# Later pairs' outputs transposed by VectorE in 32x32 blocks instead of by TensorE, in a fused attention and mixture-of-experts kernel

## The chip, the cores and the metric

The kernel runs on one core of one Trainium2 chip. The metric is device time in microseconds (us) of one execution. Before the change it is 1516.14 us, the median of 3 runs (1514.83 to 1516.44).

## The reference

Attention inside chunks of 64 tokens, then a mixture of four experts over the 4608 x 512 result, all in fp32:

```python
def _attn_ref(q, k, v):                       # (8, 8, 576, 64) each
    ...
    scores = scale * np.matmul(q_c, k_c.transpose(0, 1, 2, 4, 3))   # chunks of 64
    attn = softmax(scores)
    out = np.matmul(attn, v_c)

def _moe_ref(x, domain_probs, w1, w2):        # x (4608, 512), w1 (4, 512, 1024), w2 (4, 1024, 512)
    p = domain_probs / (domain_probs.sum(-1, keepdims=True) + 1e-09)
    for e in range(E):
        h = np.maximum(x @ w1[e], 0.0)
        out += p[:, e:e + 1] * (h @ w2[e])
```

## The kernel before

The 4608 tokens are cut into nine subs of 512 (`SUB`). The first sub is done alone, the other eight as four pairs, numbered 0 to 3. Each expert's hidden layer is cut in two halves, so there are eight passes (`n_pass`) over the weights per sub or pair: passes 0 to 7 for the first sub, 8 to 15 for pair 0, and 16 to 39 for pairs 1, 2 and 3, "the later pairs", eight each. Every fp32 factor is split into a high and a low part, and a product of two tiles is six TensorE instructions (two blocks of the inner dimension times high x high, low x high and high x low), all issued at L465 in `product`. The two products of a pair of subs use a scheme with seven products in place of eight; names such as "a11", "s1", "t4" are its sums of blocks.

In a later pair a pass is woven by hand (`WOVEN`): 28 steps, each one product. `g1` to `g7` and `h1` to `h7` make the hidden layer of this pass, from weights w1; `a1` to `a7` and `b1` to `b7` multiply the hidden layer of the pass before by w2. Their results are added by VectorE (L694) into eight SBUF tiles `acc0` to `acc7`, of 128 output columns by 512 tokens each: `acc[m + 4 s]` is the block of columns m (0 to 3) of sub s (0 or 1) of the pair. The accumulators are thus transposed against the output, which has tokens in rows. Group a makes the blocks with even m, group b those with odd m.

When a pair is done, its accumulators are transposed and stored. For pairs 1 and 2 that is woven into the first pass of the next pair and into the pass after (`outputs`, called from `later_pass`): four calls behind steps 15, 18, 21 and 24 of passes 24 and 32 for even m, and four behind steps 1, 4, 7 and 10 of passes 25 and 33 for odd m. Each call has TensorE transpose four 128x128 pieces into the PSUM tile `psa` (L780), ScalarE copy them to a stage (`e` or `pt`, L789), and SP issue two stores of 128 KB, in rows of 512 bytes (L793). The last pair has no next pass; `last_products` runs its fourteen w2 steps in the order `ALONE`, and transposes between them with `plane`: seven blocks as whole planes (four transposes, a copy by ScalarE or VectorE at L1331, a store at L1333) and the eighth, of which the last product is computed in two halves of 256 tokens (`by_halves`).

All transfers are issued by SP from one queue, in the order in which the program is written. Most are the weight factors of the later pairs: `ring_load` (L370) brings 512 KB into one of six SBUF tiles `wf0` to `wf5`, three for w1 and three for w2; the tile is used by two steps for each of its two units, and when the last of these is done it is loaded again with the unit three further on in its ring. GpSimd (POOL) makes the low parts of the hidden layer (L647), ScalarE the high parts (L644), VectorE the ReLU with the expert's share (L632) and the sums (L638, L667).

Of the kernel before, what the change touches and what calls it, by code (L numbers as in the profile page):

```python
# [8 lines left out]
F32 = mybir.dt.float32  # L9
# [6 lines left out]
P = 128  # L16
C = 64
SUB = 512
NT = SUB // P
HG = 4  # L20
GT = 2
NK = 4
# [3 lines left out]
PAIR = 2  # L26
# [4 lines left out]
def chunk_attention_moe(ctx: ExitStack, tc: tile.TileContext, qk, v, v0, dp, w1, w2, out):  # L31
# [10 lines left out]
    nc = tc.nc  # L42
# [9 lines left out]
    att = ctx.enter_context(tc.tile_pool(name="att", bufs=1))  # L52
# [6 lines left out]
    ps = ctx.enter_context(tc.tile_pool(name="ps", bufs=1, space=bass.MemoryType.PSUM))  # L59
# [5 lines left out]
    def bank(name=None):  # L65
        if name is None:
            name = BANKS[turn[0] % len(BANKS)]
            turn[0] += 1
        return ps.tile([P, SUB], F32, name=name)
# [40 lines left out]
    st = {}  # L110
# [368 lines left out]
    acc = {}  # L479
# [190 lines left out]
    class Outer:  # L670
# [17 lines left out]
        def add(self, src, i, s):  # L688
            key = self.n // n_pass, 2 * i + self.g + NK * s
            if key not in acc:  # L690
                acc[key] = opool.tile([P, SUB], F32, name=f"acc{key[1]}")
                nc.scalar.copy(out=acc[key], in_=src)
            else:
                nc.vector.tensor_tensor(out=acc[key], in0=src, in1=acc[key], op=ALU.add)  # L694
# [32 lines left out]
    class Tile:  # L727
# [25 lines left out]
        def whole(self):  # L753
            self.part(range(NK), slice(0, dm), True, True)
# [22 lines left out]
    def output_part(pair, i, m, out_ps):  # L777

        s, j = divmod(i, NT)
        nc.tensor.transpose(out_ps, acc[pair + 1, m + NK * s][:, j * P : (j + 1) * P], ident)  # L780

    def outputs(pair, i, g):

        ps = psa[:, 0].rearrange("p (i m d) -> p i m d", i=2, d=P)
        for j in range(2):
            for m in range(2):
                output_part(pair, i + j, g + 2 * m, ps[:, j, m])
        stage = att.tile([P, 2, 2, P], F32, name=("e", "pt")[i // 2 % 2])
        nc.scalar.copy(out=stage, in_=ps)  # L789
        t = (1 + pair * PAIR) * NT + i  # L790
        to = out[t * P : (t + 2) * P, :].rearrange("(i p) (m d) -> p i m d", p=P, d=P)
        for j in range(2):
            nc.sync.dma_start(out=to[:, j, g::2], in_=stage[:, j])  # L793


    scr = xpool.tile([P, NK * PAIR * SUB], F32, name="xraw")
# [386 lines left out]
        1: ((LATE, 0),), 2: ((EARLY, 1),), 3: ((EARLY, 2), (LATE, 3)), 4: ((EARLY, 4),),  # L1183
        5: ((EARLY, 5), (LATE, 6)), 6: ((EARLY, 7),),
    }
    ALONE = "a1 b1 a2 a5 b5 a6 b6 a3 b3 a7 b7 b2 a4 b4".split()

    def first_load(pair):
        if pair < n_pairs:
# [51 lines left out]
    def later_pass(n, ahead, late, held):  # L1241

        first_pass, last_pass = n % n_pass == 0, n % n_pass == n_pass - 1
        pair, more = n // n_pass - 1, n + 1 < n_run
        at = {}
        left, sc = Units(n), Scaled(n)
        steps = {"gh"[g]: LaterGroup(g, left, sc, False) for g in range(2)}
        steps |= {"ab"[g]: Outer(g, n - 1, ahead[1], ahead[0], False) for g in range(2)}

        def put(i, name, k, of=sc):  # L1250
            add(at, i, lambda: of.hi(name, k), lambda: of.lo(name, k))

        for f in held:
            add(at, 0, f)
        second_half(at, ahead[0])
        for i, f in late:
            add(at, i, f)

        add(at, 12, lambda: sc.sum("t3", 0, nc.gpsimd))
        put(16, "b11", 0)  # L1260
        put(16, "b11", 1)
        add(at, 18, lambda: sc.sum("t2", 0))
        put(19, "t2", 0)
        put(20, "b22", 0)
        add(at, 22, lambda: sc.sum("t1", 0))
        put(22, "t3", 0)
        put(23, "t1", 0)
        put(24, "b21", 0)
        put(24, "b22", 1)
        put(26, "b21", 1)  # L1270
        if more:
            add(at, 26, lambda: sc.sum("t4", 0, nc.gpsimd))
        add(at, 27, lambda: sc.sum("t1", 1), lambda: sc.sum("t3", 1))
        if n % 2 and more:
            add(at, 13, lambda: probs_load(n + 1, 0))
            add(at, 27, lambda: probs_load(n + 1, 1))
        if pair + 1 < n_pairs:
            for places, i in TILES.get(n % n_pass, ()):
                attend(at, pair + 1, places, i)
        late = []  # L1280
        if first_pass and pair > 1:
            for i in range(4):
                add(at, 15 + 3 * i, lambda i=i: outputs(pair - 1, 2 * i, 0))
            late = [(1 + 3 * i, lambda i=i: outputs(pair - 1, 2 * i, 1)) for i in range(4)]
        if last_pass and more:
            x = Tokens(pair + 1)
            add(at, 5, x.sum1)
            add(at, 8, lambda: x.sum3(nc.gpsimd), lambda: x.sum2_apart(nc.gpsimd))
            add(at, 13, x.sum4_apart)
            add(at, 15, lambda: x.hi("b11"))  # L1290
            add(at, 16, lambda: x.hi("b21"), lambda: x.lo("b11"))
            add(at, 18, lambda: x.lo("b21"))
            add(at, 20, x.split2)
            add(at, 23, lambda: x.hi("t1"))
            add(at, 24, lambda: x.lo("t1"))
            add(at, 25, lambda: x.hi("t3"))
            add(at, 26, lambda: x.hi("t4"))
            late = [
                (0, lambda: x.hi("b22")), (0, lambda: first_load(pair + 2)), (1, lambda: x.lo("t3")),
                (6, lambda: x.lo("t4")), (8, lambda: x.lo("b22")),  # L1300
            ]
        for i, name in enumerate(WOVEN):
            getattr(steps[name[0]], f"p{name[1]}")()
            for f in at.get(i, ()):
                f()
        return (sc, left), late, ()
# [11 lines left out]
    def last_products(ahead):  # L1318

        pair, at = n_pairs - 1, {}  # L1320
        second_half(at, ahead[0])
        add(at, 2, lambda: ahead[0].sum("t4", 0, nc.gpsimd))
        steps = {"ab"[g]: Outer(g, n_run - 1, ahead[1], ahead[0], True) for g in range(2)}
        stages = [(hpool, f"s{i}", 1) for i in (1, 2, 3)]
        stages += [(wpool, "wraw", N_RAW)] * 4 + [(att, "e", 1), (att, "pt", 1)]

        def store(s, m, ps, eng, rows=range(NT)):

            pool, name, bufs = stages.pop()
            stage = pool.tile([P, len(rows), P], F32, name=name, bufs=bufs)  # L1330
            eng(out=stage, in_=ps)  # L1331
            t = (1 + pair * PAIR + s) * NT + rows[0]
            nc.sync.dma_start(  # L1333
                out=out[t * P : (t + len(rows)) * P, m * P : (m + 1) * P].rearrange("(i p) d -> p i d", p=P),
                in_=stage,
            )

        def plane(s, m, ps, eng):
            ps = ps.rearrange("p (i d) -> p i d", d=P)
            for j in range(NT):  # L1340
                output_part(pair, s * NT + j, m, ps[:, j])
            store(s, m, ps, eng)

        def by_halves(o):

            left, n = o.left(1, "a22", o.g), SUB // 2
            sums = []
            for i, ps in enumerate((psa[:, 1], bank("A0"))):
                cols = slice(i * n, (i + 1) * n)
                product(ps[:, :n], PARTS, lambda k, a: left[a][:, k], lambda k, b: o.h.part("t4", b)[:, k, cols])  # L1350
                sums.append(opool.tile([P, n], F32, name=f"acc{NK + i}"))
                nc.vector.tensor_tensor(
                    out=sums[i], in0=ps[:, :n], in1=acc[o.n // n_pass, 2 + o.g][:, cols], op=ALU.add
                )
            for i, ps in enumerate((bank("A1"), bank("B1"))):
                ps = ps[:, :n].rearrange("p (i d) -> p i d", d=P)
                for j in range(n // P):
                    nc.tensor.transpose(ps[:, j], sums[i][:, j * P : (j + 1) * P], ident)
                store(0, 2 + o.g, ps, (nc.scalar.copy, nc.vector.tensor_copy)[i], range(2 * i, 2 * i + 2))

        act, dve = nc.scalar.copy, nc.vector.tensor_copy
        for i, name in enumerate(ALONE[:-1]):
            getattr(steps[name[0]], f"p{name[1]}")()
            for f in at.get(i, ()):
                f()
            if name == "b7":
                steps["b"].add(steps["b"].a, 1, 0)
            elif name == "b2":
                plane(1, 0, bank("C1"), act)
                plane(1, 1, bank("C0"), act)  # L1370
            elif name == "a4":
                plane(1, 2, psa[:, 0], act)
                plane(1, 3, bank("B1"), dve)
                plane(0, 0, bank("B0"), act)
                plane(0, 1, bank("C1"), dve)
                plane(0, 2, bank("C0"), act)
        by_halves(steps["b"])

    with tc.manual_schedule():
# [58 lines left out]
```

## Time and profile before

| | |
|---|---|
| runs shown | 1514.83, 1516.14, 1516.44 us (median 1516.14) |
| the profiled execution | 1515.59 us, of which the span from first to last instruction is 1513.8 us |
| TensorE (PE) | busy 1505.7 us, 99% of the span, 8854 matmuls |
| VectorE (DVE), ScalarE (ACT), GpSimd (POOL) | busy 918.6, 572.9, 871.7 us: 61%, 38%, 58% |
| transfers | 314.17 MB in 167936 packets, mean 208 GB/s; the SP queue's packets take 63.7% of the 16 DMA engines' time |
| granted TensorE clock | 1.00 |

The profile is of one execution, 0.55 us faster than the median of the runs shown. A matmul's row gives its own duration, but matmuls overlap: six of 128x512 follow each other in 1.36 us. The chain of work that ended last gives time without this overlap. "Packets" are the pieces of a transfer, one for each contiguous run of bytes. A group's row has its count, its busy time and the mean duration of one.

### The profile page before, as it was taken

The numbers are of one execution on the slowest core, as the hardware profiler recorded it, in microseconds if no ns is written. First come the engines' busy times: TensorE is split into PE (matmuls) and PEld (weight loads), VectorE is DVE, ScalarE is ACT, GpSimd is POOL, SyncE is SP. The second block draws the span as 40 slices with busy tenths as digits, with TensorE's granted clock in tenths as the row PEclk, the third lists the DMA queues.
The fourth block names the chain that finished last, engine by engine and source line by source line (L and its number), as shares of the span: only waits on it lengthen the run. The fifth ranks groups of instructions, "written<-read, shape, count | busy, mean of one in ns | idle before, by whom it ended". The sixth has DMA issues, their size and how long they took to land.

```text
span 1513.8 us, 23370 instructions
## 1 busy us (share of the span) xinstructions
PE 1505.7 (99%) x8854; PEld 1238.8 (82%) x8855; DVE 918.6 (61%) x1289; ACT 572.9 (38%) x1000; POOL 871.7 (58%) x666
## 2 busy tenths in 40 slices
PE   9999999999999999999999999999999999999998
PEld 7888888888888888888888888888888888888887
DVE  5443554444444465776766956666668756666665
ACT  3333444344444334333333444333333443333332
POOL 2443588677766616555556754555557555555554
PEclk9999999999999999999999999999999999999999
DMA  6443359877767576767665677676666676666664
GB/s 197 133 156 125 106 167 310 274 251 243 231 234 238 187 266 215 230 209 228 205 203 189 216 226 243 205 229 209 212 190 200 204 231 201 201 200 201 200 191 145
DMA packets 167936, 314.17 MB, mean 208 GB/s; under 512 B 14208, under 2 KB 84112, under 8 KB 167824
## 3 DMA queue, kind: packets, MB, share of 16 engines
q1 hardware_dynamic: 167824, 312.68, 63.7%
q8 instruction: 70, 1.15, 0.3%
q14 instruction: 42, 0.34, 0.1%
HBM read 244.39 MB, written 68.23 MB: 207 GB/s over the span
## 4 chain that ended last, share of the span: by engine, by line
PE 99%; DVE 0%; ACT 0%; issue 0%; ACTq 0%
PE A L465 49%; PE C L465 29%; PE B L465 16%; PE psa L169 1%; PE psa L140 1%; PE psa L160 1%; PE psa L780 0%; PE C L901 0%; PE B L852 0%; PE A L832 0%; PE C L780 0%; PE A L852 0%; PE psa L832 0%; PE B L838 0%; PE psa L838 0%; PE B L780 0%
## 5 line engine op out<-in xcount | busy, mean ns | idle before, releaser
L647 POOL TENSOR_TENSOR hfl<-wraw,hfh 128x512 fp32r<-128x512 f32 x288 | 374.4, 1316 | 216.2 <-ACT hfh L644 214.0
L465 PE MATMUL A<-xh,wf 128*128 128x512 f32 (+1 forms) x1104 | 379.5, 389 | 0.0
L465 PE MATMUL A<-hfh,wf 128*128 128x512 f32 (+1 forms) x768 | 270.6, 394 | 0.0
L644 ACT CAST hfh<-wraw 128x512 fp32r<-128x512 f32 x288 | 176.4, 622 | 208.5 <-DVE wraw L638 59.7
L465 PEld LDWEIGHTS A<-xh,wf 128*128 128x128 f32 x1104 | 206.8, 188 | 43.1
L527 ACT COPY s<-A 128x512 f32<-128x512 f32 x192 | 112.8, 587 | 329.7 <-PE A L465 328.9
L465 PE MATMUL A<-xl,wf 128*128 128x512 f32 (+1 forms) x552 | 213.7, 388 | 0.0
L465 PE MATMUL C<-xh,wf 128*128 128x512 f32 (+1 forms) x600 | 204.0, 388 | 0.7 <-ACT xh L278 0.7
L465 PEld LDWEIGHTS A<-hfh,wf 128*128 128x128 f32 x768 | 144.1, 188 | 31.0 <-DVE acc L694 1.2
L694 DVE TENSOR_TENSOR acc<-A,acc 128x512 f32<-128x512 f32 x174 | 119.2, 686 | 78.7 <-PE A L465 78.2
L465 PE MATMUL A<-hfl,wf 128*128 128x512 f32 x384 | 149.4, 389 | 0.0
L465 PE MATMUL C<-hfh,wf 128*128 128x512 f32 x384 | 133.9, 390 | 0.0
L281 POOL TENSOR_TENSOR hfl<-wraw,hfh 128x512 fp32r<-128x512 f32 x64 | 85.9, 1372 | 80.5 <-ACT hfh L278 80.5
L465 PEld LDWEIGHTS C<-xh,wf 128*128 128x128 f32 x600 | 111.5, 188 | 23.9 <-ACT xh L278 0.8
L465 PE MATMUL B<-xh,wf 128*128 128x512 f32 (+1 forms) x376 | 125.3, 384 | 0.0
L281 POOL TENSOR_TENSOR wf<-wraw,wf 128x512 fp32r<-128x512 f32 x70 | 91.5, 1330 | 53.4 <-ACT wf L278 53.2
L465 PEld LDWEIGHTS A<-xl,wf 128*128 128x128 f32 x552 | 103.5, 188 | 21.1
L465 PE MATMUL C<-xl,wf 128*128 128x512 f32 (+1 forms) x300 | 114.7, 385 | 0.0
L638 POOL TENSOR_TENSOR wf<-wraw,wf 128x512 f32<-128x512 f32 x23 | 29.7, 1291 | 145.2 <-DVE wf L632 145.2
L694 DVE TENSOR_TENSOR acc<-C,acc 128x512 f32<-128x512 f32 x90 | 62.2, 691 | 64.3 <-PE C L465 58.7
L647 POOL TENSOR_TENSOR hfl<-wf,hfh 128x512 fp32r<-128x512 f32 x48 | 71.2, 1483 | 38.9 <-ACT hfh L644 38.6
L465 PEld LDWEIGHTS C<-hfh,wf 128*128 128x128 f32 x384 | 72.1, 188 | 14.9
(186 smaller groups left out, 2727.7 us busy)
## 6 DMA issues: line engine op xcount, KB each, us to landing
wf<-w SPq DMA_DIRECT2D x336, 512.0 KB, 4.1
wraw<-in_w SPq DMA_DIRECT2D x128, 256.0 KB, 4.0
w<-wf SPq DMA_DIRECT2D x112, 256.0 KB, 4.7
qk_in<-in_qk SPq DMA_DIRECT2D x32, 512.0 KB, 5.4
v_in<-in_v SPq DMA_DIRECT2D x32, 256.0 KB, 4.4
w<-hfl SPq DMA_DIRECT2D x32, 256.0 KB, 2.7
w<-hfh SPq DMA_DIRECT2D x32, 256.0 KB, 2.9
w<-hfh SPq DMA_DIRECT2D x48, 128.0 KB, 2.7
```

Source lines behind the costliest of these rows:

```text
L140: nc.tensor.matmul(s["sc"][half, c, j], lhsT=s["x"][rows, g, 0, h], rhs=s["x"][rows, g, 1, h], start=True, stop=True,)
L160: nc.tensor.transpose(ps[:, j], s["e"][:, j].rearrange("p c k -> p (c k)"), ident)
L169: nc.tensor.matmul(av[half, c, j], lhsT=s["v"][rows, 2 * j + odd], rhs=s["pt"][rows, j, half], start=True, stop=True,)
L281: eng.tensor_tensor(out=t[1], in0=src, in1=t[0].bitcast(F32), op=ALU.subtract)
L465: nc.tensor.matmul(out, lhsT=lhs(k, a), rhs=rhs(k, b), start=first and i == 0, stop=last and i == len(parts) - 1, skip_group_check=not (fi ...
L527: nc.scalar.copy(out=t, in_=self.a)
L638: (eng or nc.vector).tensor_tensor(out=self.values[place, k], in0=self.values[a, k], in1=self.values[b, k], op=op)
L644: nc.scalar.copy(out=self.part(name, 0)[:, k], in_=self.values[name, k])
L647: (eng or nc.gpsimd).tensor_tensor(out=self.part(name, 1)[:, k], in0=self.values[name, k], in1=self.part(name, 0)[:, k].bitcast(F32), op=A ...
L694: nc.vector.tensor_tensor(out=acc[key], in0=src, in1=acc[key], op=ALU.add)
```

## The change

The transposes of `outputs` and of three blocks of the tail leave TensorE. VectorE transposes a whole accumulator (128x512) with one instruction that transposes each 32x32 block in itself (`nc.vector.transpose`, L797 and L1339 in the new kernel). The blocks then are still at the wrong place on the block level, and the store puts them right: four transfers per accumulator, one for each group of 32 partitions, in rows of 32 floats (128 bytes) in place of 128 floats (`put_out`, L789 in the new kernel). In the tail three blocks, (s, m) = (0,0), (1,0) and (1,3), go that way; (0,1), (1,2), (1,1), (0,2) and the halved (0,3) stay with TensorE. The order of the w2 steps there (`ALONE`) moves b7 and b2 ahead of a7 and b3, and the transposes of block (0,2) go between the two halves of the last product.

```diff
-    def outputs(pair, i, g):
-
-        ps = psa[:, 0].rearrange("p (i m d) -> p i m d", i=2, d=P)
-        for j in range(2):
-            for m in range(2):
-                output_part(pair, i + j, g + 2 * m, ps[:, j, m])
-        stage = att.tile([P, 2, 2, P], F32, name=("e", "pt")[i // 2 % 2])
-        nc.scalar.copy(out=stage, in_=ps)
-        t = (1 + pair * PAIR) * NT + i
-        to = out[t * P : (t + 2) * P, :].rearrange("(i p) (m d) -> p i m d", p=P, d=P)
-        for j in range(2):
-            nc.sync.dma_start(out=to[:, j, g::2], in_=stage[:, j])
+    B = 32
+
+    def put_out(pair, m, s, stage):
+
+        t = (1 + pair * PAIR + s) * SUB
+        to = out[t : t + SUB, m * P : (m + 1) * P]
+        for a in range(P // B):
+            nc.sync.dma_start(
+                out=to[:, a * B : (a + 1) * B].rearrange("(b i) j -> i b j", i=B),
+                in_=stage[a * B : (a + 1) * B].rearrange("i (b j) -> i b j", j=B),
+            )
+
+    def outputs(pair, m, s):
+
+        stage = att.tile([P, SUB], F32, name=("e", "pt")[s])
+        nc.vector.transpose(stage, acc[pair + 1, m + NK * s])
+        put_out(pair, m, s, stage)
...
-    ALONE = "a1 b1 a2 a5 b5 a6 b6 a3 b3 a7 b7 b2 a4 b4".split()
+    ALONE = "a1 b1 a2 a5 b5 a6 b6 a3 b7 b2 a7 b3 a4 b4".split()
...
             for i in range(4):
-                add(at, 15 + 3 * i, lambda i=i: outputs(pair - 1, 2 * i, 0))
-            late = [(1 + 3 * i, lambda i=i: outputs(pair - 1, 2 * i, 1)) for i in range(4)]
+                add(at, 15 + 3 * i, lambda i=i: outputs(pair - 1, 2 * (i // 2), i % 2))
+            late = [(1 + 3 * i, lambda i=i: outputs(pair - 1, 1 + 2 * (i // 2), i % 2)) for i in range(4)]
...
+        def whole(s, m):
+
+            t = stage(SUB)
+            nc.vector.transpose(t, acc[pair + 1, m + NK * s])
+            put_out(pair, m, s, t)
...
+                if i == 0:
+                    plane(0, 2, bank("C1"), act)
...
+        add(at, 3, lambda: whole(0, 0))
+        add(at, 8, lambda: steps["b"].add(steps["b"].a, 1, 0))
+        add(at, 8, lambda: whole(1, 0))
+        add(at, 9, lambda: whole(1, 3))
+        add(at, 11, lambda: plane(0, 1, psa[:, 0], act))
+        add(at, 12, lambda: plane(1, 2, bank("B0"), act))
+        add(at, 12, lambda: plane(1, 1, bank("C0"), act))
...
-            if name == "b7":
-                steps["b"].add(steps["b"].a, 1, 0)
-            elif name == "b2":
-                plane(1, 0, bank("C1"), act)
-                plane(1, 1, bank("C0"), act)
-            elif name == "a4":
-                plane(1, 2, psa[:, 0], act)
-                plane(1, 3, bank("B1"), dve)
-                plane(0, 0, bank("B0"), act)
-                plane(0, 1, bank("C1"), dve)
-                plane(0, 2, bank("C0"), act)
```

TensorE in pass 24, from the end of step 15 (h2, into bank B0) to step 16 (b1, into A1), before; `psa` is the PSUM tile of the transposes:

```order
L465 MATMUL B0_8526<-xl0_8199,wf0_8441 128x512
L465 MATMUL B0_8526<-xh0_8198,wf0_8441 128x512
L780 MATMUL psa_95<-ident_90,acc0_5723 128x128
L780 MATMUL psa_95<-ident_90,acc2_5889 128x128
L780 MATMUL psa_95<-ident_90,acc0_5723 128x128
L780 MATMUL psa_95<-ident_90,acc2_5889 128x128
L465 MATMUL A1_8544<-hfh0_8211,wf2_8398 128x512
```

Now step 16 follows step 15 with nothing between, there and at the fifteen other places. VectorE from the same step 15 on, now:

```order
L667 TENSOR_TENSOR B0_8526<-B0_8526,s1_8524 128x512
L632 SCALAR_TENSOR_TENSOR wraw_8534<-B0_8526,ws_5471 128x512
L797 STREAM_TRANSPOSE e_8536<-acc0_5723 128x512
L694 TENSOR_TENSOR acc1_5947<-A1_8542,acc1_5947 128x512
L694 TENSOR_TENSOR acc7_5962<-C1_8558,acc7_5962 128x512
L638 TENSOR_TENSOR wraw_8411<-wf6_8505,wraw_8411 128x512
L797 STREAM_TRANSPOSE pt_8577<-acc4_5831 128x512
L694 TENSOR_TENSOR acc5_5989<-A1_8542,acc5_5989 128x512
```

Before, the same rows stood there without the two L797, so each transpose now comes behind the ReLU or sum of its step and ahead of the next accumulations. SP at the same place, before, where `out_0` is the output and `w...` the weight units in memory:

```order
L370 DMA wf4_8522<-w0_0_6_102 128x1024
L793 DMA out_0<-e_8540 256x1x128 x2
L370 DMA wf2_8551<-w7_1_6_207 128x1024
L370 DMA wf0_8574<-w1_0_0_110 128x1024
L793 DMA out_0<-pt_8583 256x1x128 x2
L370 DMA wf5_8593<-w0_1_0_103 128x1024
```

and now:

```order
L370 DMA wf4_8522<-w0_0_6_102 128x1024
L789 DMA out_0<-e_8536 32x16x32 x4
L370 DMA wf2_8549<-w7_1_6_207 128x1024
L370 DMA wf0_8572<-w1_0_0_110 128x1024
L789 DMA out_0<-pt_8577 32x16x32 x4
L370 DMA wf5_8589<-w0_1_0_103 128x1024
```

Two stores have become four at the same places between the weight loads. TensorE in the tail, from the end of the last whole steps to the first half of the last product (into `psa`), before:

```order
L465 MATMUL B0_14002<-hfh1_13865,wf5_13928 128x512
L780 MATMUL C1_14010<-ident_90,acc4_11810 128x128 x4
L780 MATMUL C0_14018<-ident_90,acc5_11953 128x128 x4
L465 MATMUL A1_13902<-hfh3_13967,wf0_13789 128x512
L465 MATMUL A1_13902<-hfl3_13969,wf0_13789 128x512
...
L780 MATMUL psa_95<-ident_90,acc6_11787 128x128 x4
L780 MATMUL B1_14040<-ident_90,acc7_11932 128x128 x4
L780 MATMUL B0_14048<-ident_90,acc0_11715 128x128 x4
L780 MATMUL C1_14056<-ident_90,acc1_11917 128x128 x4
L780 MATMUL C0_14064<-ident_90,acc2_11884 128x128 x4
L465 MATMUL psa_95<-hfh3_13967,wf5_13928 128x256
```

and now, where the step into A1 is a4 again and A0 takes the second half of the last product:

```order
L465 MATMUL C0_13916<-hfh2_13782,wf4_13864 128x512
L1357 MATMUL psa_95<-ident_90,acc1_11885 128x128 x4
L465 MATMUL A1_13870<-hfh3_13941,wf0_13757 128x512
...
L1357 MATMUL B0_14010<-ident_90,acc6_11759 128x128 x4
L1357 MATMUL C0_14018<-ident_90,acc5_11921 128x128 x4
L465 MATMUL psa_95<-hfh3_13941,wf5_13896 128x256
...
L1357 MATMUL C1_14035<-ident_90,acc2_11852 128x128 x4
L465 MATMUL A0_14026<-hfh3_13941,wf5_13896 128x256
```

Seven planes have become four, one of them between the halves. VectorE in the tail now, from step b7 (into A0) on:

```order
L694 TENSOR_TENSOR acc7_11900<-A0_13879,acc7_11900 128x512
L694 TENSOR_TENSOR acc3_11999<-A0_13879,acc3_11999 128x512
L1339 STREAM_TRANSPOSE e_13962<-acc4_11782 128x512
L694 TENSOR_TENSOR acc1_11885<-B0_13968,acc1_11885 128x512
L1339 STREAM_TRANSPOSE wraw_13976<-acc7_11900 128x512
L694 TENSOR_TENSOR acc6_11759<-A1_13870,acc6_11759 128x512
```

The accumulation of step a7, the row with `acc6`, which must be done before step a4 may write on into A1, now has two transposes ahead of it.

More of the change, by code (lines that the diff above doesn't have):

```diff
@@ L1325, in last_products, with stage @@
         stages += [(wpool, "wraw", N_RAW)] * 4 + [(att, "e", 1), (att, "pt", 1)]
+        def stage(*shape):
+            pool, name, bufs = stages.pop()
+            return pool.tile([P, *shape], F32, name=name, bufs=bufs)
+        def whole(s, m):
+            t = stage(SUB)
+            nc.vector.transpose(t, acc[pair + 1, m + NK * s])
+            put_out(pair, m, s, t)
         def store(s, m, ps, eng, rows=range(NT)):
-            pool, name, bufs = stages.pop()
-            stage = pool.tile([P, len(rows), P], F32, name=name, bufs=bufs)
-            eng(out=stage, in_=ps)
+            st = stage(len(rows), P)
+            eng(out=st, in_=ps)
             t = (1 + pair * PAIR + s) * NT + rows[0]
@@ L1334, in store @@
                 out=out[t * P : (t + len(rows)) * P, m * P : (m + 1) * P].rearrange("(i p) d -> p i d", p=P),
-                in_=stage,
+                in_=st,
             )
+        act = nc.scalar.copy
         def plane(s, m, ps, eng):
@@ L1340, in plane @@
             for j in range(NT):
-                output_part(pair, s * NT + j, m, ps[:, j])
+                nc.tensor.transpose(ps[:, j], acc[pair + 1, m + NK * s][:, j * P : (j + 1) * P], ident)
             store(s, m, ps, eng)
@@ L1359, in by_halves @@
                 store(0, 2 + o.g, ps, (nc.scalar.copy, nc.vector.tensor_copy)[i], range(2 * i, 2 * i + 2))
-        act, dve = nc.scalar.copy, nc.vector.tensor_copy
+        add(at, 3, lambda: whole(0, 0))
[5 more added lines that the diff above has]
+        add(at, 12, lambda: plane(1, 1, bank("C0"), act))
         for i, name in enumerate(ALONE[:-1]):
```

## The prediction, made before the changed kernel ran

> **What bounds the kernel now.** I read the page first, then who waited for whom on TensorE, then the chain of work that ended last around the places of the change. From the page:
>
> ```profile
> span 1513.8 us, 23370 instructions
> ...
> PE 1505.7 (99%) x8854; PEld 1238.8 (82%) x8855; DVE 918.6 (61%) x1289; ACT 572.9 (38%) x1000; POOL 871.7 (58%) x666
> ```
>
> TensorE's waits in the whole span, two of six rows (the rest is smaller or start-up too):
>
> ```profile
> PE C L901 <- DVE s L895: 1.2, 1, 1.2
> ...
> PE C L465 <- ACT xh L278: 0.7, 1, 0.7
> ```
>
> TensorE is busy 99% of the span, and no row has it wait for anything in the later pairs: no factor, bank or weight comes late. So an instruction taken out of its queue there shortens the run by what it occupies, as long as nothing else comes late. What one call of `outputs` occupies, from the chain in pass 24 (start, us, what):
>
> ```profile
> 875.63 0.44 PE psa L780 x4
> 876.06 1.39 PE A L465 x6
> 877.46 1.38 PE C L465 x6
> 878.84 1.36 PE A L465 x6
> 880.20 0.44 PE psa L780 x4
> 880.63 1.38 PE A L465 x6
> 882.02 2.72 PE C L465 x12
> 884.74 0.44 PE psa L780 x4
> ```
>
> Four transposes take 0.44 us, and the products behind them 1.38 or 1.39 instead of 1.36. From group to group it is 4.57 and 4.54 us, and three undisturbed products are 3 x 1.36 = 4.08: a group costs 0.49 or 0.46, 0.475 us in the mean.
>
> **Term 1, the sixteen groups of passes 24, 25, 32 and 33.** 16 x 0.475 = 7.6 us less of TensorE. ScalarE loses sixteen copies, which gains nothing of itself.
>
> **Term 2, the tail.** The chain there:
>
> ```profile
> 1502.43 0.87 PE C L780 x8
> 1503.31 1.38 PE A L465 x6
> 1504.68 0.44 PE psa L780 x4
> 1505.12 0.87 PE B L780 x8
> 1505.99 0.87 PE C L780 x8
> ...
> 1509.29 0.42 DVE s L1331
> ```
>
> Seven planes (28 transposes) take 3.05 us, 0.44 each; three go: 1.3 us. The steps are the same fourteen. The last copy so ends at 1509.71 - 1.3 = 1508.4 on the old scale. Behind it come the stores (duration of issue in ns as minimum, median and maximum, first and last start):
>
> ```profile
> L1333 SPq DMA_DIRECT2D out<-wraw x4: 372/438/676, 1505.8 to 1507.4; - x4
> L1333 SPq DMA_DIRECT2D out<-s x3: 747/817/829, 1508.2 to 1510.0; - x3
> ...
> DMA to landing us min/median/max: 2.3/2.9/4.1
> ```
>
> The last store is issued at 1510.0, 0.3 us after its copy, because SP is held by the one before, and the issues take twice as long as earlier ones. The reason is in the transfers between 1507 and 1512:
>
> ```profile
> DMA packets 2877, 1.43 MB, mean 286 GB/s; under 512 B 95, under 2 KB 2876, under 8 KB 2876
> ...
> q1 hardware_dynamic: 2876, 1.42, 101.8%
> ```
>
> The sixteen engines are full for these 5 us: the end is bound by the drain of nine stores that come in a burst. Three blocks will have left earlier, at steps 3, 8 and 9, so the last issue need not wait: another 0.3 us. A shorter flight (2.3 instead of about 3) could add 0.7; I count 0.2. Term 2 is 1.3 + 0.3 + 0.2 = 1.8 us.
>
> **What VectorE pays.** Nineteen transposes of 128x512; no row has such an operation. Rows of that size (busy us, mean ns):
>
> ```profile
> L694 DVE TENSOR_TENSOR acc<-A,acc 128x512 f32<-128x512 f32 x174 | 119.2, 686 | 78.7 <-PE A L465 78.2
> L638 DVE TENSOR_TENSOR wraw<-wf,wraw 128x512 f32<-128x512 f32 x48 | 72.7, 1515 | 5.5 <-POOL hfl L647 4.5
> L1352 DVE TENSOR_TENSOR acc<-psa,acc 128x256 f32<-128x256 f32 x1 | 0.4, 425 | 0.4 <-PE psa L465 0.4
> ```
>
> So 0.43 us for something twice as fast, 1.5 for something that stays in SBUF and is slowed as L638 is (two SBUF inputs, with GpSimd at work). I take 0.69: a transpose has one input, as the reading of one new stream in L694. What covers it shows in three stretches: passes 24 and 25 with the outputs, and the pass behind, which has attention instead (time busy and count by engine, granted clock, DMA share, GB/s):
>
> ```profile
> 875.00:912.60 37.60, 37.60 (x183) 31.09 (x182) 21.06 (x27) 16.98 (x30) 20.79 (x16) 1.00 0.71 226
> 912.60:950.00 37.40, 37.40 (x255) 30.53 (x254) 25.23 (x37) 15.89 (x28) 22.01 (x17) 1.00 0.75 245
> ```
>
> Eight transposes add 5.5 us to VectorE's 21.06: 26.6 in 36 us, 74%, against 67% in the attention stretch, where TensorE is busy for all 37.40 us. At 1.5 us each it would be 33 of 36, too tight. Each is one step's wait at most for the accumulations behind it; a bank is written again two steps (2.7 us) after the product that the accumulation reads. I cost it at nothing. In the tail it is tighter: between b7 and a4 VectorE has four accumulations and two transposes, 6 x 0.69 = 4.1 us, in three steps and a plane, 4.5 us. At 0.69 that fits with 0.4 to spare; at 1.5 a4 starts 1.2 us late.
>
> **What the stores pay.** A block went out in 512 packets of 512 bytes, and goes out in 2048 of 128 bytes. No row has such packets. The window above prices 512 bytes: 5 us x 16 x 1.018 / 2876 = 28 ns per packet. A stretch with weight loads alone, 1450 to 1490:
>
> ```profile
> DMA packets 2111, 7.69 MB, mean 192 GB/s; under 512 B 238, under 2 KB 238, under 8 KB 2110
> ...
> q1 hardware_dynamic: 2110, 7.67, 59.7%
> ```
>
> That is 40 x 16 x 0.597 / (2110 - 238) = 204 ns for 4096 bytes. The straight line through both gives 9 ns at 128 bytes; if a packet costs the same however small, it is 28. The 204 holds queueing, so the true line is flatter and its value at 128 bytes higher: I take 14. A block then is 2048 x 14 / 16 = 1.8 us of all engines, against 0.9 before, and 3.6 at 28. Over the eight blocks of a pair the DMA share of 0.71 of 37.6 us (26.7 us) becomes 33.9 at 14 ns and 48 at 28: free of cost in the first case, over the time that there is in the second.
>
> What a late weight load may take:
>
> ```profile
> L370 SPq DMA_DIRECT2D wf<-w x336: 319/320/963, 535.7 to 1490.2; - x168
> ...
> DMA to landing us min/median/max: 3.2/4.1/7.8
> ```
>
> In `WOVEN`, the shortest way from the release of a weight buffer to the first use of its next unit is from b1 to b2, seven products between, 9.5 us; less a flight of 4.1 that leaves 5.4 us. Against that stands what SP adds. In pass 24:
>
> ```profile
> 876.10 0.59 ACT L789 COPY e<-psa 128x512 f32<-128x512 f32 x1 [1.21 <-PE psa L780]
> 876.54 0.69 DVE L632 SCALAR_TENSOR_TENSOR wraw<-B,ws 128x512 f32<-128x512 f32 x1
> 876.71 1.29 SPq L793 DMA_DIRECT2D out<-e  x2
> 878.05 2.50 SPq L370 DMA_DIRECT2D wf<-w  x2
> ```
>
> The store waited for a copy that ended at 876.69; now for a transpose that can end at 877.23 + 0.69 = 877.9, with the weight loads queued behind it on SP. Then four issues of about 0.6 us (half of 1.29 each) in place of two. The load at 878.05 goes out 2.5 us later, of 5.4 that it may. Four issues are 2.4 us of the 4.1 between calls. I cost it at nothing; without this cover each further us late would be a us of TensorE.
>
> [...]
>
> **The sum.** 7.6 + 1.8 = 9.4 us less, from 1515.59 of the profiled execution 1506.2. That execution is 0.55 below the median shown, so against the median: 1516.1 - 9.4 = 1506.7.
>
> **The rivals.** First: small packets cost what 512-byte ones cost, 28 ns. Then a pair's outputs need 48 us of transfers in 36; the weight loads fall back by some 12 us, of which the 5.4 hide, and TensorE waits for `wf` about 6.5 us per pair, 13 in both. That eats the 7.6 and more, but the wait itself gives the loads time at the end of each stretch, and part of the 0.71 is overlapped queueing: 8 rather than 13. Result 1516.1 - 9.4 + 8 = 1514.7, within 0.2%. For it: nothing prices a packet under 512 bytes. Against it: between 512 and 4096 bytes the cost follows the bytes.
>
> [...]
>
> Third: VectorE's transposes take 1.5 us. Then a4 is late by 1.2 us in the tail, and in the passes a bank is released late now and then, say 0.1 us at sixteen places: 1506.7 + 2.8 = 1509.5. For it: L638. Against it: that slowness is seen with two SBUF inputs.
>
> **How the numbers follow.** The forecast 0.72, same price for all packets 0.09, read-modify-write 0.10, slow transposes 0.09. Its own bounds: 16 x 0.49 + 2.5 = 10.3 less at best, from the lowest of the runs shown 1504.5, from the median 1505.8; at worst 8 less, 1508.1. With the third rival the range 1505.0 to 1511.5 holds 0.8. What a measurement can tell from no change is about 0.2%, 3 us. Faster: the forecast, the third rival and some of the first, 0.83; same 0.07; slower 0.10.
>
> **What would show it.** Right: no L780 in the chain between 870 and 1240, products there 1.36 us apart with no wait of TensorE for `wf`; STREAM_TRANSPOSE at about 0.69 us; a DMA share in 870 to 912 between 0.85 and 0.95; the last store issued within 0.2 us of its copy. Wrong: TensorE waiting for a transfer or for VectorE in passes 24, 25, 32, 33; stores that land later than 5 us; flights of `wf` beyond 9 us.

## The result, and the profile after

| | before | after |
|---|---|---|
| median of the five timed runs (lowest to highest) | 1515.45 us (1514.83 to 1516.44) | 1506.01 us (1505.59 to 1506.8) |
| ratio after/before, 95% interval | | 0.9938 [0.9924, 0.9952] |
| profiled execution, span | 1515.59, 1513.8 us | 1506.8, 1504.9 us |

The changed kernel is 9.4 us faster. From the page of after:

```profile
span 1504.9 us, 23273 instructions
...
PE 1497.4 (100%) x8779; PEld 1231.3 (82%) x8779; DVE 927.9 (62%) x1306; ACT 564.2 (37%) x983; POOL 871.6 (58%) x666
...
DMA packets 197775, 314.16 MB, mean 209 GB/s; under 512 B 53776, under 2 KB 113952, under 8 KB 197664
...
q1 hardware_dynamic: 197664, 312.68, 65.4%
```

TensorE has 8.3 us less to do; VectorE has 9.3 us more, the queue some 30,000 packets more, and its share of the DMA engines has risen from 63.7% to 65.4% only. Whether something new comes late is read from TensorE's waits; these are all the rows of the span:

```profile
PE A L837 <- DMA xraw<-in_qk: 1.6, 2, 0.9
PE C L906 <- DVE s L900: 1.2, 1, 1.2
PE C L465 <- ACT xh L278: 0.7, 1, 0.7
PE B L1376 <- DVE acc L1368: 0.3, 1, 0.3
```

The first three belong to the start, the last to the end of the halved block; in the later pairs there is none. The chain in pass 24, at the place shown of before (start, us, what), has products alone, 1.36 us apart:

```profile
875.19 1.36 PE B L465 x6
876.55 1.36 PE A L465 x6
877.91 1.36 PE C L465 x6
```

The transposes' source line (duration in ns as minimum, median, maximum, then first and last start) and what VectorE waited for ahead of them:

```profile
L797 DVE STREAM_TRANSPOSE e<-acc x8: 699/702/712, 878.1 to 1222.9; 128x512 f32<-128x512 f32 x8
L797 DVE STREAM_TRANSPOSE pt<-acc x8: 697/701/712, 881.7 to 1229.8; 128x512 f32<-128x512 f32 x8
...
  DMA out<-e: 2.2, 2
  DMA out<-pt: 1.3, 2
```

Each takes 0.70 us. Four of the sixteen found their stage not yet stored and waited 3.5 us together, at no cost to TensorE. The DMA share of the two stretches with outputs stands next to the end of the rows by window (time busy and count by engine, granted clock, DMA share, GB/s), and the packets of the first are counted by the view of transfers:

```profile
876.50:912.00 35.50, 35.50 (x165) 29.15 (x167) 26.66 (x36) 12.85 (x23) 20.80 (x16) 1.00 0.84 218
1195.00:1231.00 36.00, 36.00 (x160) 29.83 (x159) 25.97 (x36) 13.41 (x23) 21.15 (x17) 1.00 0.82 208
...
DMA packets 14348, 7.73 MB, mean 218 GB/s; under 512 B 12848, under 2 KB 12848, under 8 KB 14347
```

With 204 ns for each of the 1500 large packets, as before, the 12848 small ones took (35.5 x 16 x 0.84 - 1500 x 0.204) / 12848 = 13 ns each. The packets' own times in the trace say the same: 13.1 ns in the mean for the 16384 of 128 bytes between 870 and 930 us.

The tail's chain, from the last whole steps on, and the last stores:

```profile
1495.72 0.44 PE psa L1357 x4
1496.15 1.40 PE A L465 x6
1497.55 0.44 PE B L1357 x4
1497.99 0.44 PE C L1357 x4
1498.42 0.71 PE psa L465 x6
1499.14 0.44 PE C L1357 x4
1499.58 0.73 PE A L465 x6
...
1501.29 0.42 DVE s L1345
```

```profile
L1347 SPq DMA_DIRECT2D out<-s x3: 372/372/373, 1500.2 to 1501.7; - x3
...
DMA to landing us min/median/max: 2.2/2.5/3.0
```

Four planes of 0.44 us are left, the last issue starts as its copy ends (1501.71), and an issue takes 0.37 us where it took 0.82.

The traces can be cut at the same products, which gives the time of each part in us (start to pass 24, pass 24 to pass 34, pass 34 to the first of the last fourteen w2 steps, and those to the end):

| kernel | to 24 | 24 to 34 | 34 to tail | tail to end |
|---|---|---|---|---|
| before | 853.53 | 403.94 | 228.48 | 27.85 |
| after | 854.46 | 396.28 | 228.49 | 25.63 |

The passes with outputs gave 7.66 us, the tail 2.22, and passes 34 to 39 nothing. The part before pass 24, which the change does not touch, differs by up to 2.3 us between the profiled runs here; in after 1.7 us of it come from a granted clock of one half between 8.1 and 11.5 us, which the profile of before doesn't have. So the experiments are compared by the other parts.

### The profile page after: what moved, and what is told of

Read it like the earlier page. It is cut to its first block, busy times and chain, and to the rows that moved or that the text cites. A ratio compares the mean times of both kernels' runs of the same rounds, so it can differ in the third digit from the quotient of the medians.

```text
span 1504.9 us, 23273 instructions
## 1 busy us (share of the span) xinstructions
PE 1497.4 (100%) x8779; PEld 1231.3 (82%) x8779; DVE 927.9 (62%) x1306; ACT 564.2 (37%) x983; POOL 871.6 (58%) x666
## 3 DMA queue, kind: packets, MB, share of 16 engines
q1 hardware_dynamic: 197664, 312.68, 65.4%
## 4 chain that ended last, share of the span: by engine, by line
PE 99%; DMA 0%; SPq 0%; DVE 0%; ACT 0%; issue 0%
PE A L465 49%; PE C L465 29%; PE B L465 16%; PE psa L169 1%; PE psa L140 1%; PE psa L160 1%; DMA xraw<-in_qk 0%; PE C L906 0%; PE B L857 0%; PE A L837 0%; SPq L821 0%; PE A L857 0%; PE B L843 0%; PE psa L837 0%; PE psa L843 0%; PE C L1357 0%
## 5 line engine op out<-in xcount | busy, mean ns | idle before, releaser
L644 ACT CAST hfh<-wraw 128x512 fp32r<-128x512 f32 x288 | 176.5, 622 | 212.2 <-DVE wraw L638 60.7
L638 POOL TENSOR_TENSOR wf<-wraw,wf 128x512 f32<-128x512 f32 x23 | 29.7, 1292 | 144.4 <-DVE wf L632 144.4
```

The lines of the kernel that those rows point to most:

```text
L638: (eng or nc.vector).tensor_tensor(out=self.values[place, k], in0=self.values[a, k], in1=self.values[b, k], op=op)
L644: nc.scalar.copy(out=self.part(name, 0)[:, k], in_=self.values[name, k])
```

## The experiments

**1. The woven outputs alone.** After's `outputs` and `put_out` with before's tail.

```diff
 # put_out, outputs and their places in later_pass as in after; last_products and ALONE as in before
```

> The woven outputs go by VectorE as in the changed kernel, the tail is the one of before. Theory (each of the sixteen groups of four transposes was 0.475 us of TensorE that nothing else covered, 7.6 us in all, and the tail's share is separate): 7.6 us under before, so 1507.9 against 1515.5, and the profile's steps from the start of the last fourteen w2 steps to the end of the span last 27.7 us as before. Rival (the whole gain hangs on the tail or on both together): less than 6 us under before.

Measured: 1508.38 us (1507.01 to 1509.19), ratio 0.995 [0.9938, 0.9962]. Pass 24 to 34 took 396.27 us, tail to end 27.61: the first term by itself, and the old tail unchanged.

**2. The tail alone.**

```diff
 # last_products, ALONE and put_out as in after; outputs and its places as in before
```

> The tail of the changed kernel, with the woven outputs of before. Theory (three planes less, 1.3 us, and 0.9 us of store drain behind the last copy): 2.2 us under before, 1513.3 against 1515.5; 25.5 us from the start of the last fourteen w2 steps to the end of the span, against 27.7. Rival (the tail's gain is the three planes alone): 1.3 us, 1514.2.

Measured: 1513.2 us, ratio 0.9985 [0.9977, 0.9994]. Pass 24 to 34 took 403.90 us, tail to end 25.86. Against the runs of before the two parts are worth 7.0 and 2.2 us, 9.3 together, and the whole change 9.4: they add.

**3. Twice the transposes.** Is VectorE's work covered with room to spare?

```diff
         nc.vector.transpose(stage, acc[pair + 1, m + NK * s])
+        nc.vector.transpose(stage, acc[pair + 1, m + NK * s])
         put_out(pair, m, s, stage)
```

> Each woven transpose of the changed kernel is done twice, so VectorE has 16 x 0.70 = 11.2 us more. Theory (VectorE's work is covered, but the stores go out 0.7 us later and the weight loads behind them on SP had only 0.5 us to spare at the tightest place): within 1.5 us of the changed kernel, 1506.0 to 1507.5, and where TensorE waits it is for a weight load. Rival (VectorE at some 90% delays its accumulations and TensorE waits for them): over 1509, with TensorE waiting for VectorE or ScalarE.

Measured: 1507.22 us (1506.1 to 1508.09), ratio 0.9942 [0.9929, 0.9956]; pass 24 to 34 took 399.08 us, 2.80 more than in after. TensorE's waits between 860 and 1300 us, all rows:

```profile
PE B L465 <- DMA wf<-w: 0.6, 1, 0.6
PE A L465 <- DVE wraw L632: 0.6, 1, 0.6
PE C L465 <- DMA wf<-w: 0.6, 1, 0.6
```

So 0.7 us more of VectorE per block makes TensorE wait, and two of the three waits are for a weight load, which VectorE has nothing to do with directly. These rows name 1.8 of the 2.8 us. Most of the rest is overlap that a wait breaks. A row counts from the end of the matmul ahead, but undisturbed matmuls start every 0.227 us (1.36 / 6) and last 0.39. Counted from the start of the matmul ahead to the start of the third one behind the wait, less three such intervals, the three waits cost 2.65 us. (This profiled run is the slowest of the five; by the medians experiment 3 is 1.2 us slower than after.) To see how much of the loads' cover was used up, I set the landing of each weight transfer in a trace against the start of the first product that reads it, and took the least of these margins (us):

| kernel | read in 870 to 930, without the next column's | the load that step b2 of pass 25 reads (at 926 to 930) | read in 1190 to 1270 |
|---|---|---|---|
| before | 5.5 | 5.5 | 5.9 |
| after | 0.5 | 0.3 | 0.9 |
| 3, double transposes | 0.4 | 0.05 | 0.1 |

The same woven passes also ran in experiments 1 and 7, whose traces have 2.0, 0.5, 0.8 and 1.0, 0.1, 0.7 in these columns: the first moves by up to 1.5 us between executions, the other two by 0.4 or less. A margin near zero, as in experiment 3, is a wait: the product starts as the transfer has landed. After was within 0.3 us of one, and no view of its page says so, since a margin makes no wait. Experiments 8 and 9 come back to the reason.

**4. Twice the packets.** What if a block's store cost as much as the first rival said?

```diff
         put_out(pair, m, s, stage)
+        more = dram.tile([P, SUB // B, 2 * B], F32, name=f"more{pair}_{m}_{s}")
+        nc.sync.dma_start(out=more[:, :, :B], in_=stage.rearrange("p (b j) -> p b j", j=B))
```

> Behind each of the sixteen woven blocks of the changed kernel one more transfer of 2048 packets of 128 bytes goes to a scratch in memory, as if each packet of the block cost 26 ns instead of 13; SP issues five transfers per block instead of four. Theory (the weight loads' margin of 5.5 us was used up to 0.5 us): each block adds 1.7 us of engines and 0.5 us of SP, the two stretches need some 43 us of transfers in 35.5, and TensorE waits for weight tiles for some 5 to 7 us in each: 1516 to 1520. Rival (the engines' share of 0.84 is mostly overlapped queueing and the loads catch up between the blocks): under 1508.

Measured: 1525.76 us (1524.34 to 1529.45), ratio 1.007 [1.0057, 1.0083]: the direction, but far above the range expected. Pass 24 to 34 took 415.88 us, 19.6 more than in after. The waits of TensorE there, and what VectorE's transposes waited for in 870 to 960:

```profile
PE C L465 <- DMA wf<-w: 7.0, 3, 2.6
PE A L465 <- DVE wraw L632: 2.2, 2, 2.0
PE A L465 <- DMA wf<-w: 2.0, 3, 1.0
PE B L465 <- DMA wf<-w: 1.0, 1, 1.0
```

```profile
DVE pt L797 <- DMA more<-pt: 6.9, 3, 4.7
DVE e L797 <- DMA more<-e: 6.5, 2, 5.7
```

The transfers, at 2 x 2048 packets per block, don't only delay the loads in the queue: a stage comes free late, its transpose waits on VectorE, and the ReLUs and sums behind it wait with it. The listed waits come to 12.2 us of the 19.6. Part of the rest stands in the granted clock, the third number from the end of each row by window, after waits of 2.1 and 2.0 us:

```profile
918.00:920.00 2.00, 2.00 (x6) 1.54 (x6) 1.86 (x4) 0.00 (x0) 0.90 (x1) 0.50 0.97 148
920.00:922.00 2.00, 2.00 (x8) 1.60 (x7) 0.36 (x1) 1.07 (x2) 0.38 (x1) 0.68 0.89 166
```

TensorE ran at half its clock for 3.41 us. Over both stretches that happened three times, and the missing clock adds up to 5.1 us (2 us x (1 - clock), summed over the windows). Counted from start to start as in experiment 3, the nine waits cost 14.7 us rather than 12.2, and with the clock that makes 19.8, against the 19.6 measured.

**5. Stores issued by ScalarE.** Its queue instead of SP's, so that weight loads never stand behind a store.

```diff
-            nc.sync.dma_start(
+            eng.dma_start(          # eng = nc.scalar for the woven blocks
```

> The woven stores of the changed kernel are issued by ScalarE's queue, so no weight load stands behind one on SP; the packets are the same. Theory (about 2.5 of the 5 us of margin that the weight loads lost went to SP, which waits for the transpose and issues four stores ahead of them, the rest to engines filled with small packets): the tightest weight load is ready 2 us or more ahead of its use; the time is that of the changed kernel, 1506.0, unless ScalarE's copies come late behind its 2 us of issues per block. Rival (the margin was lost to the engines alone): the tightest load stays under 1 us.

Measured: 1519.35 us (1517.82 to 1521.24), ratio 1.0026 [1.0014, 1.0037]. The weight loads had 5.6 us of margin or more again, in both stretches; but pass 24 to 34 took 409.84 us, 13.6 more than in after. Two of ScalarE's waits in 870 to 930, and the two largest of TensorE:

```profile
ACT acc L692 <- DMA out<-pt: 7.7, 1, 7.7
...
ACT hfh L644 <- DVE e L797: 4.8, 1, 4.8
...
PE A L465 <- DVE acc L694: 4.6, 4, 1.5
PE C L465 <- ACT acc L692: 3.5, 2, 1.9
```

The store that waits for VectorE's transpose now holds ScalarE. Behind it stand the high parts of the hidden layer (L644) and the copies with which ScalarE begins a pair's accumulators (L692); the second row of TensorE's waits is for these copies. The longest wait, 7.7 us, wasn't VectorE's alone: the first of the four stores ahead of that copy went out at 915.77, behind its transpose, and the last at 920.37, held until a transfer had landed. TensorE's waits as listed are 9.1 us of the 13.6, and 12.0 counted from start to start; the rest was not followed further.

**6 and 7. The end without three stores,** in before and in after: is the end bound by the drain of stores?

```diff
-                plane(1, 0, bank("C1"), act)              # in before, and (1,3), (0,0)
+                plane(1, 0, bank("C1"), act, False)       # transposed and copied, not stored
...
-            put_out(pair, m, s, t)                        # in after, in whole()
```

> The kernel of before with the stores of three tail blocks, (1,0), (1,3) and (0,0), left out (these parts of the output stay unwritten); everything else is as before. Theory (the end of before is bound by the drain of nine stores): from the last copy's end to the end of the span 3.2 us instead of 4.1. Rival (it is one store's latency): 4.1 as before.

> The changed kernel with the stores of the three tail blocks that go by VectorE left out (these parts of the output stay unwritten). Theory (those stores are out before the last copies and the end is bound by the last store's latency): from the last copy's end to the end of the span 3.2 us as in the changed kernel, within 0.1. Rival (the drain still binds): 0.3 us or more less.

Measured from the end of the last copy to the end of the span: 4.09 us in before, 3.16 in experiment 6; 3.15 in after, 3.09 in experiment 7 (times 1514.03 and 1506.39 us, one execution each). Before, the burst of stores held the end up by 0.9 us; with three blocks gone early it doesn't, and leaving these out altogether gains 0.1 us at most.

**8 and 9. The stores written two steps later.** The transposes stay where they are; the four stores of a block are written 2.7 us further on, so that SP finds the transpose done; experiment 8 with one transpose per block, experiment 9 with the doubled ones of experiment 3.

```diff
-        put_out(pair, m, s, stage)
+        done_out.append((pair, m, s, stage))
...
+                add(at, 17 + 3 * i, lambda: put_out(*done_out.pop(0)))
...
+            late += [(3 + 3 * i, lambda: put_out(*done_out.pop(0))) for i in range(4)]
```

> After, with the four stores of each woven block written two steps (2.7 us) behind their transpose, so that SP comes to them when the transpose is done. Theory (the weight loads' margin in after, 0.47 and 0.85 us at the least against 5.5 before, was used up by SP's order: loads behind stores that wait for VectorE): the least margin from a weight's landing to its first use is 2 us or more in both stretches; the time stays, 1506.0 (1505.2 to 1506.8), pass 24 to 34 takes 396.3, since nothing waited. Rival (the 128-byte packets themselves hold the loads up): the margin stays under 1 us, the time the same.

> The doubled transposes of the third experiment, with the stores two steps later as in the eighth. Theory (SP's order): TensorE no longer waits for wf, pass 24 to 34 takes 396.3 to 397.0 against 399.08 in the third, since at most the one wait of 0.6 us for VectorE itself stays; the time is 1506.0 to 1506.8. Rival (VectorE's load is what counts, wherever the stores stand): 399 and 1508.7 within 0.5, the third experiment's excess over after.

Measured: 1505.67 us (1505.34 to 1505.74), ratio 0.9935 [0.992, 0.995], and 1505.76 us (1505.53 to 1506.42), ratio 0.9936 [0.9919, 0.9952]; pass 24 to 34 took 396.23 and 396.92 us. The least margins, in the three columns of the table above: 5.5, 1.5 and 2.7 us in experiment 8; 5.1, 0.8 and 2.6 in experiment 9. What SP's stores waited for in 870 to 960, the largest row of before, of after, and of experiment 8:

```profile
SPq L793 <- ACT e L789: 9.7, 4, 3.9
```

```profile
SPq L789 <- DVE e L797: 7.6, 2, 4.4
```

```profile
SPq L789 <- DVE e L797: 1.1, 2, 0.6
```

And TensorE's only wait between 860 and 1300 us in experiment 9:

```profile
PE A L465 <- DVE wraw L632: 0.3, 1, 0.3
```

The packets, the stage buffers and (in 9) VectorE's doubled work are as they were; only the place in SP's order differs. The waits for `wf` are gone, and with the doubled transposes 2.16 of the 2.80 us come back. So for the loads of the first column the margin went to SP's order: they stood behind stores that waited for VectorE, and behind what had piled up by then. SP in after, from the end of the 4.4 us wait on:

```profile
893.29 1.57 SPq L370 DMA_DIRECT2D wf<-w  x2
899.36 1.97 SPq L789 DMA_DIRECT2D out<-e  x4
901.42 0.93 SPq L370 DMA_DIRECT2D wf<-w  x2
902.44 2.28 SPq L789 DMA_DIRECT2D out<-pt  x4
904.82 4.03 SPq L370 DMA_DIRECT2D wf<-w  x2
```

From 899.36 to 919 us SP issues without a pause of more than 0.1 us. The first load at 904.82, behind eight stores and two loads, takes 3.56 us to issue, where before no weight load took more than 0.96. In before the stores waited for ScalarE even longer in total (the row of 9.7 us) and left 5.5 us, so the length of the waits alone doesn't decide; there SP had caught up, and was waiting again, soon after each block's two stores.

The load for step b2 of pass 25 is another matter, and here the theory missed: I expected 2 us or more throughout, and it has 1.5. From before to after its margin fell by 5.2 us, and the later stores gave only 1.2 of them back. The larger part is its flight: 4.3 us before, 7.7 in after and still 7.9 in experiment 8. In experiment 8 the last block's stores, three transfers for the next pair's attention and the experts' shares, and one weight load are issued in the 6 us ahead of it, and the DMA engines are busy for 0.95 of the time from 905 to 920 us, against 0.83 in before. That it queues behind these is likely, but no run tests it: in experiment 5 the same packets leave it a flight of 3.6 us, but there TensorE is late and the transfers come further apart. So the rival, a margin under 1 us whatever SP's order, falls; whether the small packets lengthen this one flight stays open.

## Why the prediction was right, point by point

The forecast was 1506.7 us, the measured median 1506.01. The decrease forecast was 9.4 us; between the medians it is 9.4. That these agree so closely is in part luck: the five runs spread over 1.6 us before and 1.2 after, and in the traces the two parts gave 7.66 + 2.22 = 9.9 us. The 0.7 us lie in the base: before's median was 1516.14 with the runs shown and is 1515.45 over the five.

- **Term 1**, 16 x 0.475 = 7.6 us: measured 7.66, in after and alone. Reading a group's price from the chain, with the slower products behind the transposes, was right; the transposes' own 0.44 us per group would have given 7.0.
- **Term 2**, 1.8 us: measured 2.2. The planes gave 1.28 of the 1.3 forecast (first tail step to last copy: 23.76 us before, 22.48 now). The way from the last copy to the end became 0.94 us shorter, where 0.3 and 0.2 were counted. The last store's issue starts 0.03 us behind its copy where it was 0.34, as forecast. The term that was mis-sized is the shorter flight: 0.7 instead of 0.2 (2.91 us before, 2.18 now; 0.1 us is lost again behind the landing), and experiments 6 and 7 show why. The burst was gone altogether, while I took only part of the 0.7 us that the flights' rows allowed.
- **VectorE**: 0.70 us for a transpose against 0.69 taken, so the third rival falls. Its cover in the woven passes holds nearly twice that: in experiment 9, at 1.4 us per block, TensorE waited for VectorE once, 0.3 us; most of what experiment 3 lost was SP's order. In the tail the accumulation ahead of a4 ended at 1495.34 and a4 began at 1496.15 us, 0.8 to spare where 0.4 was worked out.
- **Packets**: 13 ns against 14 taken. The DMA share is 0.84 and 0.82 in the stretches with outputs, and 0.80 over the 870 to 912 us that the prediction names, under the 0.85 to 0.95 expected. One of the signs set for being wrong did come: six of the 64 woven stores took longer than 5 us to land (5.8 to 6.5); TensorE waited for none of it. The first rival, at 28 ns a packet, falls.
- **The 0.10 for a read-modify-write**: no run shows one. What the traces show in its place is a 128-byte packet at 13 ns (after), less than half of the 28 of a 512-byte one (before).
- **What hides it**: this step came out right with too thin a proof. I had 5.4 us of margin and charged 2.5 for SP. The margin before was 5.5, and of it 0.3 to 0.9 was left. I followed one store and the load behind it (at 878.05, read by step b2 of pass 24), and even there the margin fell by 3.8 us, from 6.1 to 2.3. The cost is that of the worst of sixteen, when VectorE is in the middle of sums that take 1.7 us each, and SP stands for up to 4.4 us with the loads behind it and then needs some 20 us to catch up. A longer flight was charged at nothing, and took 3.4 us from the tightest load. VectorE ahead of one such transpose in after:

```profile
894.37 1.69 DVE L638 TENSOR_TENSOR wraw<-wf,wraw 128x512 f32<-128x512 f32 x1
...
896.89 1.81 DVE L638 TENSOR_TENSOR wraw<-wraw 128x512 f32<-128x512 f32 x1
898.63 0.70 DVE L797 STREAM_TRANSPOSE e<-acc 128x512 f32<-128x512 f32 x1
```

- **The first rival's price**: too low. I let 28 ns per packet cost 8 us and be even. Experiment 4, with twice the packets at 13 ns, so 26 per packet of the store, loses 19.6 us against after. (It also has the issues of the second transfer and a stage that is held longer, so it isn't that rival alone.) "Each further us late would be a us of TensorE" was wrong there: 12.2 us of listed waits came with 5.1 us of lost clock.

## What to carry to other kernels

Work that a saturated engine does only to lay data out was worth its full price on the chain here, follow-on slowdown included (7.66 us for sixteen groups, 0.48 each, where the transposes alone took 0.44), once another engine and the store's access pattern did it; read the price from the start-to-start times there. "No waits" doesn't say how near the next one is (after had none in the later pairs, and 0.3 us left at the tightest load): for a change that puts waiting instructions into a queue, line up each transfer's landing with its first use, and look at the smallest margin. A store that waits for a compute engine belongs behind that engine's finish in the issuing queue: two steps later cost nothing here and gave the loads 1 to 5 us of their cover back.

## What the runs showed of the hardware

- In experiment 4 a short stall cost more than itself: TensorE ran at half its clock three times, for 3.41 us each, from 917.8, 1242.1 and 1259.2 us on; a matmul of 128x512 then took 0.63 us instead of 0.39. The four longest idle times there, and a matmul at half clock:

```profile
912.05 0.47 PE L465 MATMUL C<-xh,wf 128*128 128x512 f32 x1 [2.11 <-DMA wf<-w]
...
917.67 0.67 PE L465 MATMUL A<-xh,wf 128*128 128x512 f32 x1 [1.98 <-DVE wraw L632]
918.13 0.63 PE L465 MATMUL A<-xl,wf 128*128 128x512 f32 x1
...
1241.43 0.47 PE L465 MATMUL C<-xh,wf 128*128 128x512 f32 x1 [2.64 <-DMA wf<-w]
...
1258.14 0.47 PE L465 MATMUL C<-xh,wf 128*128 128x512 f32 x1 [2.23 <-DMA wf<-w]
```

  Idle times of 1.98, 2.64 and 2.23 us ended 0.1, 0.7 and 1.1 us ahead of the three half clocks. The 2.11 us that end at 912.05 were followed by a clock of 1.00 up to 916, so the length of one idle time alone doesn't decide. In experiment 5, with ten waits of up to 1.9 us between 860 and 1300 us, the clock stayed at 1.00. At the start of after's profile two waits of 0.72 and 0.90 us, which end at 6.07 and 7.65 us, were followed by half the clock from 8.1 to 11.5. So these runs give no sharp bound, and what decides they do not show.
- A VectorE transpose of 128x512 in blocks of 32x32 in fp32 cost 0.70 us in after, as much as an addition with one operand in PSUM (0.69), and wasn't slowed beside GpSimd: eight of the sixteen woven ones ran while GpSimd was at work for nine tenths of the time or more, and took 0.70 to 0.71. Of the sums with two SBUF inputs (L638), one beside an idle GpSimd took 0.69 us at 896.10, and those beside a busy one up to 1.81.
- Stores of 128-byte packets cost 13 ns each on a DMA engine in after, those of 512 bytes 28 in before. Four times as many packets for the same bytes thus took 1.9 times the time (4 x 13 / 28).
